# Gate and up, groups 2 to 6: the four down row tiles of a unit stand together behind its fourth product

## The chip, the cores and the metric

The kernel runs on one core of one Trainium2 chip. The metric is the device time of one execution in microseconds. The kernel before takes 769.2 us (median of 3 runs, 769.16 to 769.42). The profiled execution, whose trace is read here, took 769.27 us; its span, from the first to the last instruction that the profile holds, is 767.5 us, so that 1.77 us lie around the span.

The engines are named as the profile names them: PE multiplies matrices and PEld loads the weights for it, DVE and ACT work on vectors in SBUF and PSUM, POOL is the general engine, SP only issues transfers here. Each runs its own instructions strictly in the order in which the program issues them.

## What is computed

Cut to what matters, with one batch of 2048 rows of 448 numbers:

```python
xn = _layernorm(x, axis=-1)
# Fourier mixing: two DFTs as matrix products, the real part kept
a = jnp.einsum("bsd,ed->bse", xn, dft_hid_re)
b = jnp.einsum("bsd,ed->bse", xn, dft_hid_im)
s = jnp.einsum("ts,bse->bte", dft_seq_re, a) - jnp.einsum("ts,bse->bte", dft_seq_im, b)
# gated feed-forward, 448 -> 1792 -> 448
h = (_gelu(xn @ w_gate) * (xn @ w_up)) @ w_down
out = x + s * _silu(h)
```

The change lies in the gated feed-forward.

## The kernel before

Products keep their accuracy by splitting each factor into a high part, rounded to the type that PE reads, and a low part that holds the rest; three products (high by high, high by low, low by high) stand for one (`three`, `two`).

**Stages.** The 1792 hidden columns are cut into 14 tiles of 128, taken in seven groups of two. Group 0 is computed plainly while x is normalised and turned. Groups 1 to 6 run in the loop over `gi`, some 326 us in the middle of the span. After it come the DFT along the hidden dimension and the DFT along the sequence.

**A unit.** In each of the groups 1 to 6 four units follow each other (`bi` from 0 to 3). A unit is one call of `strassen`: one tile of 128 hidden columns for two blocks of 512 rows, gate and up together, by a scheme that forms sums of the weights and of x beforehand and so needs fewer products. Its 39 matmuls on 512 columns are seven products: four on fresh PSUM banks, called `x1` to `x4`, with six matmuls each, and three second parts of five matmuls each, which add to the banks of `x1`, `x3` and `x4`. These four banks are 0 to 3 of the eight, and each unit uses the same ones in the same order, so a unit's `x4` can begin only after the bank has been read by the unit before.

Between the products stand DVE and ACT instructions that move results on. At the end of a unit they form a chain: DVE adds the second part of `x3` (L525) and multiplies by the gelu of `x1` (L526); ACT copies the product as a high part `hs` (L528); DVE forms its low part (L530); DVE adds the second part of `x4` (L534), which is the last reading of that bank; ACT takes the gelu of the sum (L535). What is left (L539 on DVE, L541 on ACT, L544 on DVE) is returned as `late` and issued in the next unit.

**Down row tiles.** The second product, with `w_down`, is spread over later units: eight pieces for each pair of units wait in the queue `dq`, and `send` takes one of them. A piece (`down_one`) is six matmuls on 448 columns into a PSUM bank of the other four (4 to 7), then an ACT copy into `po_out` (L457). Behind the fourth copy POOL issues the transfer that adds `po_out` to `gs` in HBM (L462, 896 KB). `strassen` gets four calls, `dn[0]` to `dn[3]`, and issues them behind its second product, behind its fourth, behind the second part of `x3` and at its end. In the groups 2 to 6 each of them is a `send`.

**Preparation of weights.** `preps` holds four lists of work for later units, issued at four fixed places. In the units `bi` 0 and 3 of the groups 2 to 5, and `bi` 0 of group 6, `preps[1]` and `preps[2]` each split one half of the next weights (`prep_s`): an ACT copy of 896 columns (L356) and DVE subtractions (L358, L362). In the units `bi` 2 they split `w_down` for the next group (an ACT copy L384, then a DVE subtraction L385). `preps[1]` stands behind the fourth product, `preps[2]` behind the gelu of `x1` (L521).

**POOL.** At the beginning of the units `bi` 1 and `bi` 2 of the groups 2 to 5 the program issues `sums_s` on POOL: ten additions and subtractions on 128 columns in SBUF (L338 to L347), which form the sums of the next group's weights. At the end of every third unit `sum_step` has POOL issue two transfers that add DFT matrices in HBM (L809). So what POOL does in its order is: a unit's `gs` transfer, the two transfers of `sum_step` where they are due, and then the ten instructions of the next unit's `sums_s` where it has them. SP loads the raw weights; its load for a raw buffer waits until the buffer's last reader, the DVE subtraction of `preps[2]`, has finished.

Of the kernel before, what the change touches and what calls it, by code (L numbers as in the profile page):

```python
# [45 lines left out]
def fnet_geglu(ctx: ExitStack, tc: tile.TileContext, x, ca, ct, cp, et, wgu, wd, out):  # L46
# [45 lines left out]
    def tmp(i):  # L92
        return a_t[:, 512 * i : 512 * i + 512]
# [7 lines left out]
    def xk(c, k, lo=0):  # L101
        at = k if c % 2 == 0 else (0, 2, 1, 3)[k]
        return a_x[c][:, 2048 * lo + 512 * at :][:, :512]
# [31 lines left out]
    def mm_tile(name):  # L135
        return in_turn("mm", name)
# [162 lines left out]
    def load_s(f, i):  # L299
        raw = a_r[i]  # L300
        nc.sync.dma_start(raw[:, :1280], wgu[f].rearrange("p b f -> p (b f)"))
        return raw
# [108 lines left out]
    def new_hs(f, c):  # L411
        hs_of[f, c] = hs_tile()
        return hs_of[f, c]
# [56 lines left out]
    def three(ps, a, b, first=False):  # L470

        for n, (i, j) in enumerate(((0, 0), (0, 1), (1, 0))):
            nc.tensor.matmul(  # L473
                ps, a[i], b[j], start=first and n == 0, stop=n == 2, skip_group_check=True
            )

    def two(ps, a, b):

        for xt in b:
            nc.tensor.matmul(ps, a[0], xt, start=False, stop=True, skip_group_check=True)  # L480

    def strassen(f, p, w, late, dn, preps):


        c, e = 2 * p, 2 * p + 1
        m, u, g1, c21 = [tmp(i) for i in ((0, 1, 2, 3), (2, 3, 0, 1))[units_n[0] % 2]]
        units_n[0] += 1

        def hl(c, k):
            return xk(c, k), xk(c, k, 1)  # L490

        t, v = t_hl[p]

        def bank(i):
            return mm_tile(f"x{i}_{f}_{p}")

        x1 = bank(1)
        three(x1, w["a11"], hl(c, 0), True)
        three(x1, w["b11"], hl(c, 2))
        nc.scalar.activation(m, x1, AF.Copy)  # L500
        late[0]()
        x2 = bank(2)
        three(x2, w["s2"], t[1], True)
        three(x2, w["r2"], v[1])
        nc.vector.tensor_add(u, m, x2)
        late[1]()
        dn[0]()
        preps[0]()
        x3 = bank(3)
        three(x3, w["s3"], t[2], True)  # L510
        three(x3, w["r3"], v[2])
        nc.vector.tensor_add(m, u, x3)  # L512
        x4 = bank(4)
        three(x4, w["s1"], t[0], True)
        three(x4, w["r1"], v[0])
        nc.vector.tensor_add(m, m, x4)
        preps[1]()
        dn[1]()
        three(x1, w["a12"], hl(c, 1))
        two(x1, w["x2"], hl(c, 3))  # L520
        nc.scalar.activation(g1, x1, AF.Gelu_apprx_tanh)  # L521
        preps[2]()
        three(x3, w["a22"], t[3])
        two(x3, w["x3"], v[3])
        nc.vector.tensor_add(c21, u, x3)  # L525
        nc.vector.tensor_mul(g1, g1, c21)  # L526
        hs = new_hs(f, c)
        nc.scalar.activation(hs[:, 0], g1, AF.Copy)  # L528
        dn[2]()
        nc.vector.tensor_sub(hs[:, 1], g1, hs[:, 0])  # L530
        preps[3]()
        three(x4, w["s4"], hl(e, 1))
        two(x4, w["x4"], hl(e, 3))
        nc.vector.tensor_add(u, u, x4)  # L534
        nc.scalar.activation(u, u, AF.Gelu_apprx_tanh)  # L535
        dn[3]()

        def late0():
            nc.vector.tensor_mul(u, u, m)  # L539
            late0.hs = new_hs(f, e)  # L540
            nc.scalar.activation(late0.hs[:, 0], u, AF.Copy)  # L541

        def late1():
            nc.vector.tensor_sub(late0.hs[:, 1], u, late0.hs[:, 0])  # L544

        return late0, late1

    units_n = [0]


    with tc.manual_schedule():
# [263 lines left out]
        def send():  # L815
            if dq:
                down_one(*dq.pop(0))

        nop = lambda: None

        e_at, e_raw = {}, {}

        def e_load(b):
            e_raw[b] = a_r[0][:, 960 * (b % 2) :][:, : 2 * D]
            nc.sync.dma_start(e_raw[b], et[b].rearrange("p r d -> p (r d)"))
# [17 lines left out]
        for gi in range(1, len(GROUPS)):  # L843
            grp = GROUPS[gi]
            nxt = GROUPS[gi + 1] if gi + 1 < len(GROUPS) else None
            ws = nws
            if gi > 1:
                wdn = nwdn
            nws, n_raw = [None, None], {}
            sides = (0, 0, 1, 1) if gi % 2 else (1, 1, 0, 0)  # L850
            for bi, (i, p) in enumerate(zip((0, 1, 1, 0), sides)):
                preps = [[], [], [], []]
                if gi == 1 and bi == 0:
                    tsp, vsp = t_places(1), v_places(1)
                    preps[0].append(lambda: (comb1.pop(0)(), vsp(3)))
                    preps[2].append(lambda: comb1.pop(0)())
                    preps[3].append(lambda: comb1.pop(0)())
                if gi == 1 and bi == 1:
                    comb1.pop(0)()
                    for n, f, k in ((0, vsp, 1), (1, tsp, 1), (2, tsp, 2), (3, vsp, 2), (3, tsp, 0)):  # L860
                        preps[n].append(lambda f=f, k=k: f(k))
                if gi == 1 and bi == 2:
                    vsp(0)
                    tsp(3)
                if bi == 0:
                    if gi == 1:
                        sums_s(s_raw2, nc.gpsimd)
                        n_raw[-1] = s_raw2
                    else:
                        n_raw[-1] = last_raw  # L870
                    ws[1], steps = prep_s(nw, n_raw[-1])
                    preps[1].append(steps[0])
                    preps[2].append(steps[1])
                    if nxt and gi > 1:
                        n_raw[0] = load_s(nxt[0], 0)
                    elif not nxt:
                        e_load(0)
                        e_load(1)
                elif bi == 1:
                    if nxt:  # L880
                        n_raw[1] = load_s(nxt[1], 1)
                        if gi > 1:
                            n_raw["d"] = load_d(nxt, a_s)
                            sums_s(n_raw[0], nc.gpsimd)
                        else:
                            wdn, steps = prep_d(grp, draw)
                            preps[1] += steps
                    else:
                        E_IN[0] = sb.tile([P, 1920], FR, name="e0", tag="r1")
                        preps[1].append(lambda: (e_split(0, E_IN[0]), e_load(2)))  # L890
                elif bi == 2:
                    if nxt:
                        if gi == 1:
                            n_raw["d"] = load_d(nxt, a_s)
                            n_raw[0] = load_s(nxt[0], 0)
                            sums_s(n_raw[0], nc.gpsimd)
                        sums_s(n_raw[1], nc.gpsimd)
                        nwdn, steps = prep_d(nxt, n_raw["d"])
                        preps[1].append(steps[0])
                        preps[2].append(steps[1])  # L900
                    else:
                        fetch(1)
                        E_IN[1] = sb.tile([P, 4 * D], FR, name="e1", tag="d1")
                        E_IN[2] = sb.tile([P, 2240], FR, name="e2", tag="sp")
                        preps[1].append(lambda: (e_split(1, E_IN[1]), e_load(3)))
                        preps[3].append(lambda: e_split(2, E_IN[2]))
                else:
                    if nxt:
                        nws[0], steps = prep_s(nw, n_raw[0])
                        preps[1].append(steps[0])  # L910
                        preps[2].append(steps[1])
                    else:
                        preps[1].append(lambda: e_split(3, vt[1][:, 7 * D :]))
                dn = [send] * 4
                if gi == 1 and bi < 2:
                    dn = [nop, send, nop, send]
                run = [lambda q=q: [f() for f in q] for q in preps]
                late = strassen(grp[i], p, ws[i], late, dn, run)
                sum_step(4 * gi + bi - 4)
                if bi % 2:  # L920
                    dq += [(gi, c, wdn, kk) for c in (2 * p, 2 * p + 1) for kk in range(4)]
            nw = 1 - nw
            if nxt:
                last_raw = n_raw[1]
# [117 lines left out]
        nxt = {0: 3, 1: 6, 2: 7, 3: 8, 9: None, 10: None}  # L1042
# [366 lines left out]
```

## Time and profile before

| What | Value |
|---|---|
| median of 3 runs | 769.2 us (769.16 to 769.42) |
| profiled execution | 769.27 us |
| its span | 767.5 us |
| granted TensorE clock, mean | 0.999 |
| PEld busy | 686.2 us (89%) |
| DVE busy | 544.4 us (71%) |
| ACT busy | 366.6 us (48%) |
| POOL busy | 179.9 us (23%) |
| all transfers | 170.04 MB, mean 222 GB/s |

A row of a timeline gives the start of an instruction in us from the span's start, its length in us, the engine, the line of the program and what it writes and reads. A row of the chain of waits gives a start, a length and what ran then on the path that ended last. The groups 1 to 6 lie between 71.8 and 397.8 us of the span.

### The profile page before, as it was taken

The numbers are of one execution on the slowest core, as the hardware profiler recorded it, in microseconds if no ns is written. First come the engines' busy times: TensorE is split into PE (matmuls) and PEld (weight loads), VectorE is DVE, ScalarE is ACT, GpSimd is POOL, SyncE is SP. The second block draws the span as 40 slices with busy tenths as digits, with TensorE's granted clock in tenths as the row PEclk, the third lists the DMA queues.
The fourth block names the chain that finished last, engine by engine and source line by source line (L and its number), as shares of the span: only waits on it lengthen the run. The fifth ranks groups of instructions, "written<-read, shape, count | busy, mean of one in ns | idle before, by whom it ended". The sixth has DMA issues, their size and how long they took to land.

```text
span 767.5 us, 11360 instructions
## 1 busy us (share of the span) xinstructions
PE 761.3 (99%) x4054; PEld 686.2 (89%) x4054; DVE 544.4 (71%) x946; ACT 366.6 (48%) x547; POOL 179.9 (23%) x303
## 2 busy tenths in 40 slices
PE   8999999999999999999999999999999999999998
PEld 7988888888888888888889999999999999999997
DVE  7879877555556556455452777978888797979787
ACT  5975554444444344344444585534444444434341
POOL 2204043430501511501011001223222222323130
PEclk9999999999999999999999999999999999999999
DMA  8234458994959968774979981959696969688794
GB/s 298 91 120 150 145 203 172 263 186 104 266 107 252 272 117 225 172 157 84 257 218 240 372 346 54 325 170 334 210 354 205 346 202 343 211 304 268 256 312 153
DMA packets 61513, 170.04 MB, mean 222 GB/s; under 512 B 7440, under 2 KB 40080, under 8 KB 60560
## 3 DMA queue, kind: packets, MB, share of 16 engines
q0 software_dynamic: 13728, 61.02, 35.0%
q1 hardware_dynamic: 34272, 82.48, 30.5%
q10 hardware_dynamic: 13456, 25.81, 9.2%
q8 instruction: 32, 0.52, 0.3%
q14 instruction: 25, 0.20, 0.1%
HBM read 127.21 MB, written 70.91 MB: 258 GB/s over the span
## 4 chain that ended last, share of the span: by engine, by line
PE 99%; DVE 0%; issue 0%; DVEq 0%
PE x L473 24%; PE p L1173 22%; PE po L450 18%; PE p L1176 10%; PE ab L984 9%; PE x L480 4%; PE gu L396 4%; PE py L1188 1%; PE py L1190 1%; PE py L1189 1%; PE gu L599 1%; PE pt L198 1%; PE warm L573 1%; PE p L1206 0%; PE gu L585 0%
## 5 line engine op out<-in xcount | busy, mean ns | idle before, releaser
L473 PE MATMUL x<-xt,w 128*128 128x512 f32 x480 | 149.6, 392 | 0.0
L473 PEld LDWEIGHTS x<-xt,w 128*128 128x128 f32 x480 | 90.1, 188 | 16.3 <-DVE tmp L512 0.7
L457 ACT ACTIVATE po_out<-po 128x448 f32<-128x448 f32 x112 | 60.2, 537 | 81.7 <-PE po L450 79.5
L450 PE MATMUL po<-wd0h,hs 128*128 128x448 f32 x256 | 81.7, 366 | 0.0
L462 POOL DMA_DIRECT2D gs<-po_out x24 | 21.4, 893 | 218.7 <-ACT po_out L457 213.7
L984 PE MATMUL ab<-e,xt 128*128 128x448 f32 x288 | 68.8, 365 | 0.0
L450 PE MATMUL po<-wd,hs 128*128 128x448 f32 x288 | 66.0, 365 | 0.0
L473 PE MATMUL x<-t_v,w 128*128 128x512 f32 x216 | 60.8, 390 | 0.0
L450 PEld LDWEIGHTS po<-wd,hs 128*128 128x128 f32 x288 | 54.1, 188 | 6.7
L984 PEld LDWEIGHTS ab<-e,xt 128*128 128x128 f32 x288 | 54.1, 188 | 4.3
L450 PEld LDWEIGHTS po<-wd0h,hs 128*128 128x128 f32 x256 | 48.1, 188 | 4.9
L473 PEld LDWEIGHTS x<-t_v,w 128*128 128x128 f32 x216 | 40.6, 188 | 8.7
L1064 POOL DMA_DIRECT2D raw<-sums x45 | 24.8, 552 | 94.9 <-DVE xt L143 56.6
L450 PE MATMUL po<-wd0l,hs 128*128 128x448 f32 x128 | 46.9, 367 | 0.0
L142 ACT ACTIVATE e<-raw 128x896 fp32r<-128x896 f32 (+1 forms) x30 | 27.6, 921 | 38.6 <-DVE raw L1071 27.8
L528 ACT ACTIVATE hs<-tmp 128x512 fp32r<-128x512 f32 x24 | 15.2, 634 | 54.6 <-DVE tmp L526 54.6
L473 PE MATMUL x<-t_lo,w 128*128 128x512 f32 x96 | 37.4, 389 | 0.0
L142 ACT ACTIVATE e<-tmp 128x896 fp32r<-128x896 f32 (+1 forms) x22 | 19.7, 896 | 35.7 <-DVE tmp L1071 28.6
L1173 PE MATMUL p<-t_v,wd0l 128*128 128x448 f32 x112 | 36.4, 374 | 0.0
L1173 PE MATMUL p<-w,e 128*128 128x448 f32 x112 | 36.4, 374 | 0.0
L1064 POOL DMA_DIRECT2D tmp<-sums x39 | 21.5, 552 | 59.9 <-DVE xt L143 37.2
L358 DVE TENSOR_TENSOR w<-raw,w 128x512 fp32r<-128x512 f32 (+1 forms) x24 | 21.3, 888 | 18.3 <-ACT w L356 18.3
(374 smaller groups left out, 2017.6 us busy)
## 6 DMA issues: line engine op xcount, KB each, us to landing
gs<-po_out POOLq DMA_DIRECT2D x24, 896.0 KB, 7.8
sums<-ca SPq DMA_DIRECT2D x16, 896.0 KB, 11.2
sums<-ca POOLq DMA_DIRECT2D x16, 896.0 KB, 14.5
t_v<-td ACTq DMA_DIRECT2D x24, 448.0 KB, 5.8
w<-td ACTq DMA_DIRECT2D x24, 448.0 KB, 7.5
raw<-ct SPq DMA_DIRECT2D x45, 192.0 KB, 4.2
raw<-wgu SPq DMA_DIRECT2D x12, 640.0 KB, 5.9
tmp<-ct SPq DMA_DIRECT2D x39, 192.0 KB, 4.6
```

The lines of the kernel that those rows point to most:

```text
L142: nc.scalar.activation(h, src, AF.Copy)
L358: nc.vector.tensor_sub(w[:, 1408 + lo : 1408 + b], raw[:, P + lo : P + b], hw[:, lo:b].bitcast(F32))
L396: nc.tensor.matmul(ps[:, cols], a, xt[:, cols], start=n == 0, stop=n == len(mm) - 1)
L450: nc.tensor.matmul(po[:, :D], hs[:, a, kk * P : (kk + 1) * P], wdn[b][:, i], start=n == 0, stop=n == 5,)
L457: nc.scalar.activation(out_[0][:, kk], po[:, :D], AF.Copy)
L462: nc.gpsimd.dma_start(gv[:, 4 * c : 4 * c + 4], out_[0], accum_op=ALU.add)
L473: nc.tensor.matmul(ps, a[i], b[j], start=first and n == 0, stop=n == 2, skip_group_check=True)
L480: nc.tensor.matmul(ps, a[0], xt, start=False, stop=True, skip_group_check=True)
L984: nc.tensor.matmul(p[:, :D], a, b, start=n == 0, stop=n == len(mm) - 1)
L1064: nc.gpsimd.dma_start(v[:, 4 * P : 6 * P], sums[j][:, KS.index(k)])
L1173: nc.tensor.matmul(ps[q][:, :D], h, v, start=u % UN == 0, stop=False, skip_group_check=True)
L1176: nc.tensor.matmul(ps[q][:, :HD], l, v[:, :HD], start=False, stop=u % UN == NS - 1, skip_group_check=True,)
```

## The change

The calls of `down_one` stay the same in number, kind and order; four of them now stand in one place. In the units concerned `dn[0]`, `dn[2]` and `dn[3]` do nothing and `dn[1]` calls `send` four times, behind the fourth product. Where `dn[0]` is the function `nop`, `preps[2]` is issued ahead of `dn[1]`, right behind `preps[1]`. Group 1 keeps its order (the `lambda: None` in its first units is another function than `nop`, so the test does not hold there), and so do the last three units of group 6. That leaves 17 changed units: all 16 of the groups 2 to 5 and the first of group 6.

```diff
         preps[1]()
+        if dn[0] is nop:
+            preps[2]()
         dn[1]()
         three(x1, w["a12"], hl(c, 1))
         two(x1, w["x2"], hl(c, 3))
         nc.scalar.activation(g1, x1, AF.Gelu_apprx_tanh)
-        preps[2]()
+        if dn[0] is not nop:
+            preps[2]()
...
     units_n = [0]
+    nop = lambda: None
...
-        nop = lambda: None
...
-                dn = [send] * 4
-                if gi == 1 and bi < 2:
-                    dn = [nop, send, nop, send]
+                dn = [nop, lambda: [send() for _ in range(4)], nop, nop]
+                if gi == 1 or (bi and not nxt):
+                    dn = [send] * 4 if gi > 1 or bi > 1 else [lambda: None, send, nop, send]
```

On PE, in the first unit of group 2 (its banks are `x_4_1_1225` for `x1`, then one each for `x2` to `x4`; `po_2_0` to `po_2_3` are its four row tiles), the kernel before has this behind its second product:

```order
L450 MATMUL po_2_0_1244<-wd_78,hs_80 128x448 x3
L450 MATMUL po_2_0_1244<-wd_78,hs_79 128x448 x3
L473 MATMUL x_4_1_1252<-xt_69,w 128x512
L473 MATMUL x_4_1_1252<-t_lo,w 128x512
L473 MATMUL x_4_1_1252<-xt_69,w 128x512
L473 MATMUL x_4_1_1252<-t_v_822,w 128x512 x3
L473 MATMUL x_4_1_1260<-xt_69,w 128x512
L473 MATMUL x_4_1_1260<-t_lo,w 128x512
L473 MATMUL x_4_1_1260<-xt_69,w 128x512
L473 MATMUL x_4_1_1260<-t_v_822,w 128x512 x3
L450 MATMUL po_2_1_1271<-wd_78,hs_80 128x448 x3
L450 MATMUL po_2_1_1271<-wd_78,hs_79 128x448 x3
```

And the changed kernel has this from the last rows of its fourth product on:

```order
L473 MATMUL x_4_1_1252<-xt_69,w 128x512
L473 MATMUL x_4_1_1252<-t_v_822,w 128x512 x3
L450 MATMUL po_2_0_1265<-wd_78,hs_80 128x448 x3
L450 MATMUL po_2_0_1265<-wd_78,hs_79 128x448 x3
L450 MATMUL po_2_1_1273<-wd_78,hs_80 128x448 x3
L450 MATMUL po_2_1_1273<-wd_78,hs_79 128x448 x3
L450 MATMUL po_2_2_1281<-wd_78,hs_80 128x448 x3
L450 MATMUL po_2_2_1281<-wd_78,hs_79 128x448 x3
L450 MATMUL po_2_3_1289<-wd_78,hs_80 128x448 x3
L450 MATMUL po_2_3_1289<-wd_78,hs_79 128x448 x3
L473 MATMUL x_4_1_1225<-xt_68,w 128x512 x3
```

The four groups of six matmuls on 448 columns have become one group of 24; the 24 matmuls of the four fresh products now follow each other, and so do the 15 of the second parts with the 24 of the next unit.

On ACT, in the same unit, from the copy of `x1` to that of the next unit's `x1`, the kernel before has:

```order
L500 ACTIVATE tmp<-x_4_1_1225 128x512
L541 ACTIVATE hs_80<-tmp 128x512
L457 ACTIVATE po_out<-po_2_0_1244 128x448
L356 ACTIVATE w<-raw_75 128x896
L457 ACTIVATE po_out<-po_2_1_1271 128x448
L521 ACTIVATE tmp<-x_4_1_1225 128x512
L356 ACTIVATE w<-raw_75 128x896
L528 ACTIVATE hs_80<-tmp 128x512
L457 ACTIVATE po_out<-po_2_2_1295 128x448
L535 ACTIVATE tmp<-tmp 128x512
L457 ACTIVATE po_out<-po_2_3_1311 128x448
L500 ACTIVATE tmp<-x_5_1_1332 128x512
```

And the changed kernel (the gelu of `x1`, L521 before, is L523 now; L528, L535 and L541 are L531, L538 and L544):

```order
L500 ACTIVATE tmp<-x_4_1_1225 128x512
L544 ACTIVATE hs_80<-tmp 128x512
L356 ACTIVATE w<-raw_75 128x896 x2
L457 ACTIVATE po_out<-po_2_0_1265 128x448
L457 ACTIVATE po_out<-po_2_1_1273 128x448
L457 ACTIVATE po_out<-po_2_2_1281 128x448
L457 ACTIVATE po_out<-po_2_3_1289 128x448
L523 ACTIVATE tmp<-x_4_1_1225 128x512
L531 ACTIVATE hs_80<-tmp 128x512
L538 ACTIVATE tmp<-tmp 128x512
L500 ACTIVATE tmp<-x_5_1_1332 128x512
```

The second copy of weights has moved ahead of all four copies of row tiles, and the fourth copy, for which POOL's `gs` transfer waits, has moved from the end of the unit to a place ahead of the gelu of `x1`.

On POOL the order of instructions is the same in both kernels. This is its piece from the `gs` transfer of the third group's second unit to its `sums_s`, as it stands in both:

```order
L462 DMA gs<-po_out 128x1792
L338 TENSOR_TENSOR raw_75<-raw_75 128x128
L339 TENSOR_TENSOR raw_75<-raw_75 128x128
L340 TENSOR_TENSOR raw_75<-raw_75 128x128
L341 TENSOR_TENSOR raw_75<-raw_75 64x128
L342 TENSOR_TENSOR raw_75<-raw_75 128x128
```

Nothing has moved within POOL's order, nor within those of DVE and SP. What has moved is the ACT copy for which the first of these rows waits.

## The prediction

> **What bounds the kernel now.** I read the page first: the engines' busy time, then the chain that ended last.
>
> ```profile
> PE 761.3 (99%) x4054; PEld 686.2 (89%) x4054; DVE 544.4 (71%) x946; ACT 366.6 (48%) x547; POOL 179.9 (23%) x303
> PE 99%; DVE 0%; issue 0%; DVEq 0%
> ```
>
> PE is the bound everywhere, and it waits for nobody. So this change can gain only what the spacing of matmuls gives, and it loses whatever makes PE wait. The next view is the chain in order of time, for the length of a unit.
>
> ```profile
> 71.78 5.44 PE x L473 x24
> ...
> 108.44 2.74 PE x L473 x12
> ...
> 122.36 2.74 PE x L473 x12
> ...
> 136.14 2.74 PE x L473 x12
> ...
> 149.91 2.74 PE x L473 x12
> ...
> 402.29 4.86 PE po L450 x24
> ```
>
> The units that begin at 122.36 and 136.14 last 13.78 and 13.77 us. Their ideal is in the same rows: 24 matmuls on 512 columns take 5.44 us where nothing stands between (0.2267 each), so 39 take 8.84; 24 on 448 columns in one piece take 4.86. Together 13.70.
>
> **The gain in spacing.** The difference, some 0.07 us, is paid at the changes between the two lengths:
>
> ```profile
> 130.27 0.70 PE x L473 x3
> 130.97 0.46 PE x L480 x2
> 131.42 0.68 PE x L473 x3
> 132.10 0.45 PE x L480 x2
> ```
>
> The five matmuls behind a row tile take 1.16 us, the next five 1.13: a return from 448 to 512 columns costs about 0.03 us, partly given back inside the short row tile. A unit returns four times now and once afterwards. I take 8.84 + 4.86 + 0.03 = 13.73 for the changed unit: 0.04 less. Bounds from the same rows: 0 (if a long piece pays at its end what four short ones pay) to 0.07. 17 units by 0.04 make **0.7 us of gain** (0 to 1.2).
>
> **What else moves.** The matmuls, copies and transfers are the same in number. I place everything in a changed unit by its start on PE: four fresh products to 5.44, row tiles to 10.30, second parts of `x1`, `x3`, `x4` to 11.46, 12.60 and 13.73. The next unit's `x1` needs its bank at 13.73, its `x4` at 13.73 + 4.08 = 17.81. These rows price the rest:
>
> ```profile
> 205.51 0.53 ACT L457 ACTIVATE po_out<-po 128x448 f32<-128x448 f32 x1
> 206.44 0.90 POOL L462 DMA_DIRECT2D gs<-po_out  x1 [5.44 <-ACT po_out L457]
> 207.07 0.77 POOL L338 TENSOR_TENSOR raw<-raw 128x128 f32<-128x128 f32 x1
> ...
> 208.34 0.74 POOL L341 TENSOR_TENSOR raw<-raw 64x128 f32<-64x128 f32 x1
> 208.46 2.84 DVE L544 TENSOR_TENSOR hs<-tmp,hs 128x512 fp32r<-128x512 f32 x1
> ...
> 209.43 0.94 ACT L384 ACTIVATE wd0h<-xf 128x896 fp32r<-128x896 f32 x1
> ...
> 210.01 0.72 POOL L345 TENSOR_TENSOR raw<-raw 128x128 f32<-128x128 f32 x1
> ...
> 214.10 0.60 ACT L521 ACTIVATE tmp<-x 128x512 f32<-128x512 f32 x1 [0.61 <-PE x L480]
> 215.23 0.69 DVE L525 TENSOR_TENSOR tmp<-tmp,x 128x512 f32<-128x512 f32 x1 [1.55 <-PE x L480]
> 216.03 0.69 DVE L526 TENSOR_TENSOR tmp<-tmp 128x512 f32<-128x512 f32 x1
> 216.75 0.64 ACT L528 ACTIVATE hs<-tmp 128x512 fp32r<-128x512 f32 x1 [2.05 <-DVE tmp L526]
> 217.42 0.69 DVE L530 TENSOR_TENSOR hs<-tmp,hs 128x512 fp32r<-128x512 f32 x1 [0.70 <-ACT hs L528]
> ```
>
> *ACT.* The second weight copy (0.94, as L384 on the same size) goes ahead of the row tiles' copies; both fit before the first tile ends at 6.66. A copy (0.53) comes every 1.22 us, so ACT keeps up: the fourth runs from 10.30 to 10.83. The gelu of `x1` starts at 11.46 and ends at 12.06, 1.67 us before PE wants that bank. Cost nothing; if ACT were over 1.5 us late, PE would wait at `x1`. The DVE subtraction behind the moved copy is finished earlier too, and SP's next raw load, which waits for it, starts earlier; nobody is waiting for that load.
>
> *The chain at the unit's end.* Before, two row tiles (2.4 us) of the second parts' time covered it. Now DVE's L525 starts when `x3` ends, 12.60. L526 follows 0.80 later (216.03 less 215.23), to 14.09; L528 14.12 to 14.76; L530 14.79 to 15.48. L534, the last reader of the bank of `x4`, starts 0.61 behind L530's start:
>
> ```profile
> 148.55 0.69 DVE L530 TENSOR_TENSOR hs<-tmp,hs 128x512 fp32r<-128x512 f32 x1 [0.70 <-ACT hs L528]
> 149.16 0.68 DVE L534 TENSOR_TENSOR tmp<-tmp,x 128x512 f32<-128x512 f32 x1
> ```
>
> So it ends at 16.08, and PE may go on some 0.2 later:
>
> ```profile
> 116.62 0.67 DVE L512 TENSOR_TENSOR tmp<-tmp,x 128x512 f32<-128x512 f32 x1
> 117.35 0.19 PEld L473 LDWEIGHTS x<-xt,w 128*128 128x128 f32 x1 [0.28 <-DVE tmp L512]
> 117.35 0.50 PE L473 MATMUL x<-xt,w 128*128 128x512 f32 x1
> ```
>
> Here, in group 1, a weight load did wait for DVE (ended 117.29), and the unit that begins at 108.44 took 13.92 instead of 13.78: released at 117.35 + 0.14 = 117.49. So an undisturbed chain frees the bank at 16.28, 1.53 us before 17.81: hidden, with less cover than before.
>
> *POOL, the term that decides.* POOL's `gs` transfer waits for the fourth copy. Before, that copy stood at the unit's end, and `sums_s` ran early in the next unit. Now L462 starts 0.40 behind 10.83 (206.44 less 206.04), at 11.23, and L338 0.63 later, at 11.86. `sums_s` has moved into the chain. What that does is in the first row block: DVE's L544, which reads two SBUF tiles, came 1.39 us after L338 began and took 2.84 instead of 0.69; it ended 0.57 after L345, 4.23 after L338. L526 and L530 read two SBUF tiles too. L526 now wants to start at 13.40, 1.54 after L338: the same place in POOL's sequence. Priced by that row it ends at 11.86 + 4.23 = 16.09, L528 runs to 16.76, L530 to 17.48, L534 to 18.08, PE is free at 18.28: **0.47 us of wait** at the next `x4`.
>
> This holds at boundaries where the next unit has `sums_s` and no transfers of `sum_step` stand ahead: five of the eight (behind `bi` 0 of groups 2, 4, 5 and `bi` 1 of groups 3, 4). At the other three L338 comes later and begins slowly:
>
> ```profile
> 151.30 0.88 POOL L462 DMA_DIRECT2D gs<-po_out  x1 [6.67 <-ACT po_out L457]
> ...
> 153.00 1.41 POOL L338 TENSOR_TENSOR raw<-raw 128x128 f32<-128x128 f32 x1
> 153.36 0.69 DVE L544 TENSOR_TENSOR hs<-tmp,hs 128x512 fp32r<-128x512 f32 x1
> ...
> 154.48 0.75 POOL L340 TENSOR_TENSOR raw<-raw 128x128 f32<-128x128 f32 x1
> ...
> 156.59 0.71 POOL L345 TENSOR_TENSOR raw<-raw 128x128 f32<-128x128 f32 x1
> ```
>
> 1.70 after L462: 12.93. L526 at 13.40 comes 0.47 behind it, and L544 at 0.36 passed undisturbed, so L526 ends at 14.09 and L530 wants to start at 14.79, 1.86 after L338, when L340 has begun (1.48 after it). If it is held to L345 (4.30 after L338, 17.23) and ends 0.57 later, at 17.80, L534 ends 0.60 after that, PE is free at 18.60: 0.79 us. Bounds for each boundary: 0, if DVE gets in at once, to 2.2, if L526 is held so late too.
>
> The page "SBUF — State Buffer" of the Trainium skill, section "Who interferes with whom", says that a DVE instruction with two SBUF inputs contends with a GpSimd instruction that reads SBUF, and that the loser waits for the whole instruction. The trace agrees that they contend (2.84 for 0.69), but there the wait outlasted five POOL instructions, not one. By the page's lock of one instruction the wait would be 0.4 us and the time that of the second rival.
>
> *Other waits.* Queued behind the held L526 on DVE stand L530, L534 and the next unit's L539, L505, L544 and L512, and through them ACT's L535, L500 and L541. All run some 2 to 3 us late, but of these PE needs L534 first; the others release banks or `tmp` tiles that it wants from the second parts on, at 10.30 of the next unit. The rows of `hs` that the tiles read are complete by 17.48, and the next unit's tiles begin at 13.73 + 5.44. The `gs` transfer starts about 5 us earlier in the unit, so its buffer, needed two units later, is free earlier. Behind `bi` 2 and 3 no `sums_s` follows: no wait there.
>
> **The sum.** 769.27 of the profiled execution (the median is 769.2) − 0.7 + 5 × 0.47 + 3 × 0.79 = 769.27 − 0.7 + 2.35 + 2.37 = **773.3 us**, 0.5% slower. With each wait uncertain by some 0.15 us, this case lies between 772.1 and 774.6.
>
> **Rivals.**
> 1. *Only five boundaries wait.* At the three with transfers L530 slips in. For it:
>
> ```profile
> 112.72 0.47 POOL L339 TENSOR_TENSOR raw<-raw 128x128 f32<-128x128 f32 x1
> 112.78 0.95 DVE L539 TENSOR_TENSOR tmp<-tmp 128x512 f32<-128x512 f32 x1 [0.70 <-ACT tmp L535]
> ```
>
> An arrival during L339 was held only 0.26 us, and 1.86 after a slow L338 is near the end of L339. 769.27 − 0.7 + 2.35 = 770.9.
> 2. *No wait, not slower.* DVE gets in behind one POOL instruction (0.4 us, as in these two rows). The mechanism decides at one point: a chain held less than 1.53 us stays hidden. Then only the spacing is left: 769.27 − 0.7 = 768.6. Against it: L544's 2.84 at nearly the same distance from L338 as L526 will have.
> 3. *Both L526 and L530 meet POOL at the three.* L526 held to 17.80 gives L528 to 18.47, L530 to 19.19, L534 to 19.79, free at 19.99: 2.18 each. 769.27 − 0.7 + 2.35 + 6.54 = 777.5. Against it: the 0.69 of the L544 at 0.36.
> 4. *The order doesn't reach the chip as written.* The rows of the order exclude it, so the only open part is the spacing gain, 0 to 1.2, which is inside the other cases.
>
> **How the numbers follow.** Forecast 773.3: 0.50. Rival 1: 0.17; rival 2: 0.20; rival 3: 0.07; the rest 0.06, half of it a gain beyond 0.2% from spacing I can't see. About 0.2% (1.5 us) is what a measurement of this kernel can tell from no change. Rival 1 lies at that edge, so half of it counts as the same. Faster 0.04, same 0.28, slower 0.68. The range runs from rival 2 to the upper end of the forecast, 768.4 to 774.6, and leaves out 0.13.
>
> **What would show it.** In the changed trace: row tiles as one piece of 24 in 4.86 and undisturbed units of 13.73 (the gain); L338 at 11.9 or 12.9 of the units `bi` 0 and 1; the multiplication (L529 there) or the subtraction behind it taking over 2 us; PEld waiting for DVE's last addition (L537 there) at `x4` of the units `bi` 1 and 2, eight times, 0.4 to 0.9 each; units `bi` 2 to 3 and 3 to 0 without waits. I am wrong if these DVE instructions stay near 0.7 us beside `sums_s`, or if PE waits at `x1` for the gelu instead.

## The result and the profile after

The changed kernel takes 775.56 us (median of 6 runs, 775.42 to 776.08). The kernel before takes 769.20 us beside it, the median of five runs (769.16 to 769.6); a sixth run of it took 1112.59 us and is left out of the comparison. The ratio is 1.0083, with a 95% interval of 1.0072 to 1.0094: 0.8% slower. The forecast was 773.3 us, with a range to 774.6: the sign and the mechanism came out, the size did not.

The page of the changed kernel, its busy times and the chain that ended last by engine:

```profile
PE 763.3 (99%) x4054; PEld 686.0 (89%) x4054; DVE 557.5 (72%) x946; ACT 371.3 (48%) x547; POOL 179.8 (23%) x303
PE 93%; DVE 5%; ACT 1%; issue 0%; DVEq 0%
```

The chain was PE alone; now 5% of it is DVE. These 5% are not the loss: at each boundary, the place where one unit ends and the next begins, the path runs over DVE for some 4.7 us, but PE works through most of that. PE's share of the span still rounds to 99%, for 6 us are 0.8% of it: the share alone would not show them. The view of waits, for the weight loads in the groups 2 to 6 (line, releaser, total us, times, longest), names them:

```profile
PEld x L473 <- DVE tmp L537: 8.2, 8, 1.4
```

Eight waits, all for the last DVE addition of a unit (L537 here, L534 before), as many as there are boundaries with POOL's sums behind them. The chain in order of time (start, length, what; this view leaves out the shortest pieces, among them here ACT's copy L531 and the addition L537):

```profile
122.13 5.46 PE x L473 x24
127.59 4.87 PE po L450 x24
...
134.79 0.70 DVE tmp L528
135.58 2.63 DVE tmp L529
138.90 0.71 DVE hs L533
140.26 1.67 PE x L473 x6
141.93 4.86 PE po L450 x24
...
165.22 5.44 PE x L473 x24
170.66 4.86 PE po L450 x24
...
178.95 5.44 PE x L473 x24
```

The unit from 165.22 to 178.95 has nothing behind it and lasts 13.73 us, 0.04 less than before, with its 24 row tile matmuls in one piece of 4.86. Between the row tiles at 127.59 and those at 141.93, with a boundary between them, lie 14.34 us. How that comes about, by the timeline around this boundary (start, length, engine, line, what it writes and reads, idle time before it and who ended it):

```profile
133.39 0.88 POOL L462 DMA_DIRECT2D gs<-po_out  x1 [7.41 <-ACT po_out L457]
...
133.96 0.79 POOL L338 TENSOR_TENSOR raw<-raw 128x128 f32<-128x128 f32 x1
...
135.58 2.62 DVE L529 TENSOR_TENSOR tmp<-tmp 128x512 f32<-128x512 f32 x1
...
136.93 0.71 POOL L345 TENSOR_TENSOR raw<-raw 128x128 f32<-128x128 f32 x1
...
138.24 0.63 ACT L531 ACTIVATE hs<-tmp 128x512 fp32r<-128x512 f32 x1 [3.98 <-DVE tmp L529]
...
138.90 0.71 DVE L533 TENSOR_TENSOR hs<-tmp,hs 128x512 fp32r<-128x512 f32 x1 [0.70 <-ACT hs L531]
...
139.12 0.84 PE L473 MATMUL x<-t_v,w 128*128 128x512 f32 x3
139.54 0.67 DVE L537 TENSOR_TENSOR tmp<-tmp,x 128x512 f32<-128x512 f32 x1
...
140.26 0.19 PEld L473 LDWEIGHTS x<-xt,w 128*128 128x128 f32 x1 [0.72 <-DVE tmp L537]
140.26 0.50 PE L473 MATMUL x<-xt,w 128*128 128x512 f32 x1 [0.30 <-DVE tmp L537]
...
140.60 0.40 PE L473 MATMUL x<-t_lo,w 128*128 128x512 f32 x1
```

POOL's sums start 0.57 us behind the start of the `gs` transfer, the multiplication L529 comes 1.62 us after L338 and takes 2.62 us instead of 0.69, and ends 0.56 after L345. What follows it is as long as ever. The weight load of the next `x4` stands 0.72 us. Of the other kind of boundary, where two POOL transfers stand ahead of the sums, these rows of the timeline behind the first unit of group 3:

```profile
191.94 1.74 POOL L338 TENSOR_TENSOR raw<-raw 128x128 f32<-128x128 f32 x1
...
192.37 1.73 POOL L339 TENSOR_TENSOR raw<-raw 128x128 f32<-128x128 f32 x1
192.38 0.99 DVE L529 TENSOR_TENSOR tmp<-tmp 128x512 f32<-128x512 f32 x1
...
194.07 3.05 DVE L533 TENSOR_TENSOR hs<-tmp,hs 128x512 fp32r<-128x512 f32 x1 [0.70 <-ACT hs L531]
...
195.85 0.72 POOL L345 TENSOR_TENSOR raw<-raw 128x128 f32<-128x128 f32 x1
...
197.77 0.19 PEld L473 LDWEIGHTS x<-xt,w 128*128 128x128 f32 x1 [1.43 <-DVE tmp L537]
```

There L529 slips through, and the subtraction L533 is held, as forecast; but L529 itself took 0.99, and the slow L338 1.74 instead of 1.41.

### The profile page after: what moved, and what is told of

It reads as the page before. It is cut to its first block, busy times and chain, and to the rows that moved or that the text cites. A ratio compares the mean times of both kernels' runs of the same rounds, so it can differ in the third digit from the quotient of the medians.

```text
span 773.7 us, 11369 instructions
## 1 busy us (share of the span) xinstructions
PE 763.3 (99%) x4054; PEld 686.0 (89%) x4054; DVE 557.5 (72%) x946; ACT 371.3 (48%) x547; POOL 179.8 (23%) x303
## 4 chain that ended last, share of the span: by engine, by line
PE 93%; DVE 5%; ACT 1%; issue 0%; DVEq 0%
PE p L1176 21%; PE x L473 19%; PE po L450 18%; PE p L1179 10%; PE ab L987 9%; PE gu L396 4%; PE x L480 4%; DVE tmp L529 2%; DVE hs L533 2%; PE py L1191 1%; PE py L1193 1%; PE py L1192 1%; PE gu L603 1%; PE pt L198 1%; PE warm L577 1%; DVE tmp L528 1%
## 5 line engine op out<-in xcount | busy, mean ns | idle before, releaser
L450 PE MATMUL po<-wd0h,hs 128*128 128x448 f32 x256 | 78.0, 367 | 0.0
L528 DVE TENSOR_TENSOR tmp<-tmp,x 128x512 f32<-128x512 f32 x24 | 16.5, 686 | 73.4 <-PE x L480 73.4
L450 PE MATMUL po<-wd,hs 128*128 128x448 f32 x288 | 61.8, 365 | 0.0
L531 ACT ACTIVATE hs<-tmp 128x512 fp32r<-128x512 f32 x24 | 15.2, 632 | 61.6 <-DVE tmp L529 61.6
L533 DVE TENSOR_TENSOR hs<-tmp,hs 128x512 fp32r<-128x512 f32 x24 | 25.4, 1057 | 16.8 <-ACT hs L531 16.8
```

What stands on the lines that cost most here:

```text
L450: nc.tensor.matmul(po[:, :D], hs[:, a, kk * P : (kk + 1) * P], wdn[b][:, i], start=n == 0, stop=n == 5,)
```

## The experiments

Their times stand beside the kernel before, run on the same chip. It took 769.08 us beside four of them (all sums held back, transfers ahead, another order, second preparation back) and 769.15 us beside the other three. The changed kernel was not run again beside them: its 775.56 us is that of the first measurement.

**Holding POOL's sums back.** A one-element copy on POOL waits for a DVE result of the running unit, and the sums stand behind it:

```diff
+        def sums_late(raw, hs):
+            nc.gpsimd.tensor_copy(gate, hs[:, 1, :1].bitcast(F32))
+            sums_s(raw, nc.gpsimd)
...
-                            sums_s(n_raw[0], nc.gpsimd)
+                            preps[0].append(lambda r=n_raw[0], v=late: sums_late(r, v[0].hs))
...
-                        sums_s(n_raw[1], nc.gpsimd)
+                        if gi > 1:
+                            preps[0].append(lambda r=n_raw[1], v=late: sums_late(r, v[0].hs))
+                        else:
+                            sums_s(n_raw[1], nc.gpsimd)
```

> The changed kernel, with POOL's ten sums of weights in the units bi 1 and 2 of groups 2 to 5 held back by a one-element POOL copy that reads the low part hs finished some 5 us into the unit; nothing else moves. Theory A (the end-of-unit chain on DVE is held by POOL's sums): the eight waits of the weight load for L537 vanish, L529 and L533 take 0.7 us, all changed units last 13.73 us, and the time is 775.56 - 7.1 = 768.5 us, 0.1% under the kernel before. Theory B (the chain is late of itself, because the second parts of the products now follow each other without row tiles between, or because of the gs transfer that now starts there): the eight waits stay, 775.5 us.

Measured: 768.44 us, 0.9993 of before (0.9984 to 1.0002), and no wait of a weight load in the groups 2 to 6. The timeline at the same boundary behind the first unit of group 3:

```profile
189.01 2.00 POOL L813 DMA_DIRECT2D sums<-ca  x2
...
190.55 0.69 DVE L529 TENSOR_TENSOR tmp<-tmp 128x512 f32<-128x512 f32 x1
...
191.94 0.69 DVE L533 TENSOR_TENSOR hs<-tmp,hs 128x512 fp32r<-128x512 f32 x1 [0.70 <-ACT hs L531]
...
196.08 0.19 POOL L848 COPY gate<-hs 128x1 f32<-128x1 f32 x1 [5.07 <-DVE hs L547]
...
196.22 0.46 POOL L338 TENSOR_TENSOR raw<-raw 128x128 f32<-128x128 f32 x1
```

The transfers still run at that place, and L529 and L533 take 0.69 beside them. So neither the transfers nor the closer order of the products makes the waits; the sums do. Theory B falls.

**Holding back half of them.** Only the first line of that edit, for the sums behind the units `bi` 0.

> The changed kernel, with only the sums that run behind the units bi 0 held back (those issued at the start of bi 1 of groups 2 to 5); those behind bi 1 stay in the chain. Theory A: the four waits in the units bi 1 vanish (0.59, 1.28, 0.65 and 0.63 us in the changed kernel), the four in the units bi 2 stay: 775.56 - 3.15 = 772.4 us. If the waits had a common cause beside the sums, the time would not fall by just these four.

Measured: 772.71 us, 1.0045 of before (1.0031 to 1.0059), and 2.85 less than the changed kernel for 3.15 expected; the view of waits for the weight loads of the groups 2 to 6:

```profile
PEld x L473 <- DVE tmp L537: 4.4, 4, 1.4
```

Four waits are gone and four stay. In the two traces the last unit of group 6 starts 3.27 us earlier; some 0.4 us of that is lost again behind the groups; why is open. The waits add up boundary by boundary.

**The DFT sums' transfers ahead of the unit.**

```diff
-        def sum_step(at):
+        def sum_step(at, which=(0, 2)):
...
-            for d in (0, 2):
+            for d in which:
...
+                ahead = dn[0] is nop
+                if ahead:
+                    sum_step(4 * gi + bi - 4, (2,))
                 late = strassen(grp[i], p, ws[i], late, dn, run)
-                sum_step(4 * gi + bi - 4)
+                sum_step(4 * gi + bi - 4, (0,) if ahead else (0, 2))
```

> The changed kernel, with the two POOL transfers of sum_step issued ahead of a changed unit instead of behind it, so that none stand between the gs transfer and the sums. Theory A: the three boundaries with 1.28 us of wait become like the other five (some 0.65 us each), because L338 starts at 11.8 of the unit and not at 12.9, L529 instead of L533 is held, and no slow L338 adds its 0.3 us: 775.56 - 3 x 0.63 = 773.7 us. Theory B': the longer wait of these three comes from the DFT sums' transfers loading the DMA queues: it stays 1.28, 775.5 us.

Measured: 773.65 us, 1.0059 of before (1.0045 to 1.0073). The view of waits for the weight loads, as above, and the timeline behind the first unit of group 3:

```profile
PEld x L473 <- DVE tmp L537: 6.3, 8, 0.8
```

```profile
190.25 0.81 POOL L338 TENSOR_TENSOR raw<-raw 128x128 f32<-128x128 f32 x1
...
191.80 2.70 DVE L529 TENSOR_TENSOR tmp<-tmp 128x512 f32<-128x512 f32 x1
```

Still eight waits, but the longest is 0.8 instead of 1.4: without the transfers L338 is as quick as elsewhere, and this boundary is like the other five. The edit takes the transfers away from this place and lets the sums begin earlier, so by itself it does not part the two. The first experiment speaks for the sums: there the transfers run at their old place, and L529 and L533 take 0.69 beside them. Whether the transfers slow the sums themselves is not shown.

**The same sums in another order.** In the kernel's order only the last two of the ten depend on the one just before; here seven do, because they read its result or overwrite what it reads.

```diff
         eng.tensor_sub(s3, g0, u0)
-        eng.tensor_sub(s7, g2, u2)
         eng.tensor_add(u0, u0, u1)
-        eng.tensor_add(u2[:64], u2[:64], u3[:64])
         eng.tensor_sub(s2, u0, g0)
-        eng.tensor_sub(s6, u2, g2)
         eng.tensor_sub(s4, g1, s2)
+        eng.tensor_sub(s7, g2, u2)
+        eng.tensor_add(u2[:64], u2[:64], u3[:64])
+        eng.tensor_sub(s6, u2, g2)
         eng.tensor_sub(u2d, g2d, u2d)
```

> The changed kernel, with the ten sums of weights in another order, so that all but two of them need the result of the one just before; same work, same place. Theory A1 (DVE is shut out only by a stream of POOL instructions that run into each other, and gets in at the first gap): the first gap comes after one or two instructions, L529 and L533 are held under 1 us each, the waits fall under 0.2 us: 768.5 to 769.5 us. Theory A2 (POOL keeps the port for the whole series whatever its gaps): waits of 0.6 to 1.3 us stay, 775 to 776 us.

Measured: 768.34 us, 0.9989 of before (0.9980 to 0.9998): the best kernel here, and faster than the kernel before by just about what can be told. No weight load waits in the groups 2 to 6. The timeline behind the first unit of group 4:

```profile
244.68 0.46 POOL L339 TENSOR_TENSOR raw<-raw 128x128 f32<-128x128 f32 x1
...
245.22 0.46 POOL L340 TENSOR_TENSOR raw<-raw 128x128 f32<-128x128 f32 x1
...
245.34 0.89 DVE L529 TENSOR_TENSOR tmp<-tmp 128x512 f32<-128x512 f32 x1
...
245.77 0.79 POOL L341 TENSOR_TENSOR raw<-raw 128x128 f32<-128x128 f32 x1
...
246.52 0.46 POOL L342 TENSOR_TENSOR raw<-raw 128x128 f32<-128x128 f32 x1
...
246.93 0.69 DVE L533 TENSOR_TENSOR hs<-tmp,hs 128x512 fp32r<-128x512 f32 x1 [0.70 <-ACT hs L531]
247.06 0.89 POOL L343 TENSOR_TENSOR raw<-raw 64x128 f32<-64x128 f32 x1
```

L339, L340 and L341 now lie 0.54 to 0.55 apart with 0.08 between them, and the sums run in the middle of the chain as they do in the changed kernel. L529 arrives during L340, is held 0.2 us and gets in ahead of L341, which takes 0.79 instead of 0.46.

Is that gain the new order's own? The kernel before, with this order and nothing else:

> The kernel before, with the ten sums in the chained order and nothing else. The order of the sums alone should be worth nothing in the units of groups 2 to 6 (no wait there to remove): 769.1 us, the same as the kernel before; at most 0.3 us less from group 1, where DVE was held at L530 and L544. If instead it comes out at 768.3 us, the gain of the chained run was not the regrouping's.

Measured: 769.1 us, 0.9998 of before (0.9989 to 1.0007). The order alone is worth nothing that can be measured; it is worth 7.2 us where the row tiles stand together. Its effect on DVE shows here too: the L544 that took 2.84 us in the trace before, 1.39 behind L338, comes at the same distance and takes 0.69:

```profile
208.28 0.69 DVE L544 TENSOR_TENSOR hs<-tmp,hs 128x512 fp32r<-128x512 f32 x1
```

**The second preparation back in its place**, the row tiles still together:

```diff
         preps[1]()
-        if dn[0] is nop:
-            preps[2]()
         dn[1]()
...
-        if dn[0] is not nop:
-            preps[2]()
+        preps[2]()
```

> The changed kernel, with the second preparation of weights back behind the gelu of x1 in all units; the four row tiles stay together. Theory A: in the units bi 0 the DVE subtraction of weights (two SBUF inputs, wanted at 13.0 of the unit) now meets POOL's sums and stands ahead of the whole chain in DVE's order: the waits behind bi 0 grow from 0.65 and 1.28 to some 2.4 us each, with a part of them at x3 (its bank is read by L525); behind bi 3 a wait of about 0.1 us appears: 775.56 + 3 x 1.75 + 1.2 + 0.4 = 782 us. Rival: the preparation's place costs nothing, because the sums hold the chain to the same end anyway: 775.5 us.

Measured: 782.34 us, 1.0171 of before (1.0152 to 1.0190). The view of waits for the weight loads, and two rows of the timeline behind the first unit of group 2:

```profile
PEld x L473 <- DVE tmp L534: 8.8, 8, 2.8
PEld x L473 <- DVE w L358: 6.3, 3, 2.1
```

```profile
135.12 3.46 DVE L358 TENSOR_TENSOR w<-raw,w 128x896 fp32r<-128x896 f32 x1 [5.62 <-ACT w L356]
...
138.64 0.30 PEld L473 LDWEIGHTS x<-xt,w 128*128 128x128 f32 x2 [2.05 <-DVE w L358]
```

The weights' subtraction, 1.09 us undisturbed, is now the one that is held, ahead of the whole chain in DVE's order. The time came out as expected, but one of the waits did not: at three boundaries PE stands first at the sixth matmul of the next unit's `x1`, which needs the weights that L358 forms, and then again at `x4`; the bank of `x3` had been named for the first of these. Behind `bi` 3 no wait appears (0.1 was expected). So the preparation's move, priced at nothing in the prediction, is worth 6.8 us once the tiles stand together.

**The change without any sums behind it**, in nine units:

```diff
-                if gi == 1 or (bi and not nxt):
+                if gi == 1 or (bi and not nxt) or (nxt and bi < 2):
```

> The change in nine units only: bi 2 and 3 of groups 2 to 5 and bi 0 of group 6, none of which has sums of weights behind it; the units bi 0 and 1 of groups 2 to 5 as in the kernel before. Theory A: no waits, each of the nine units 0.04 us shorter: 0.36 us under the kernel before, 768.7 to 768.9 us. If standing together had a cost of its own beside the sums, the time would be above the kernel before.

Measured: 768.86 us, 0.9995 of before (0.9986 to 1.0003). The gain of 0.29 us is near the 0.36 that nine times 0.04 let expect, but within what the measurement can't tell from nothing. What carries the spacing term is the trace: every undisturbed changed unit in all these runs lasts 13.73 to 13.75 us, against 13.77 before.

## Why the prediction was wrong in size

**Spacing.** Right: 13.73 us for the unit as worked out, and 768.34 and 768.44 us where it stands alone (768.6 forecast, as the second rival's time).

**Where the waits are.** Right: eight, at `x4` of the units `bi` 1 and 2, none elsewhere; L529 held at five boundaries, L533 at three. Rivals 1 and 2 let DVE in behind one POOL instruction; it waited until a series of them had passed.

**When DVE is done at the five.** Nearly right: at the boundary shown, L537 ends at 140.21, which is 18.08 after the start of the unit at 122.13 on the scale of the chain, as forecast. At the other four it ends 18.10 to 18.18 after the unit's start, less what that unit was itself delayed: over the five 0.05 late on average.

**The term that was mis-sized at all eight: when PE asks.** The prediction put the need of `x4` at 17.81 and added 0.2 for the release, 0.47 us in all. The five cost 0.59 to 0.71, 0.65 on average: 0.18 more each. 17.81 is on the scale of the chain, in which a piece of PE begins where the matmul before *ends*. But a matmul lasts 0.39 at a spacing of 0.23, so the next one starts 0.16 before that, and its weight load, which does the waiting, about one spacing earlier still. The rows above show it: the load stood idle from 140.26 − 0.72 = 139.54, and its matmul was due at 139.80 (139.12 and three spacings), 17.67 after the unit's start and not 17.81. The matmul behind that one is at 140.60 in the trace, so the late one went on at 140.37, 0.16 after L537's end: 0.57 late, and 0.02 more at the return to speed. The release of 0.2 had been about right. In sum 0.14 for the earlier need, less 0.04 for the release, and 0.02: 0.12 at every boundary, 1.0 us over the eight. DVE's 0.05 at the five adds 0.3.

**The term that was mis-sized at three: how L529 fares beside L338.** It was taken as undisturbed (0.69), as L544 had been in the trace before, which came 0.36 after L338. L529 came 0.44 after it, and in these 0.08 us L339 had started; it took 0.99, L338 1.74 instead of 1.41, and the whole series came later. L345 ends 4.63 after L338 instead of 4.30, L533 with it, and L537 is done 0.36 later than forecast. That it is L339 which held L529, the fourth experiment shows at the same boundary. There L339 stays back for L338, and L529 at the same distance takes 0.69:

```profile
189.97 1.44 POOL L338 TENSOR_TENSOR raw<-raw 128x128 f32<-128x128 f32 x1
190.41 0.69 DVE L529 TENSOR_TENSOR tmp<-tmp 128x512 f32<-128x512 f32 x1
...
191.48 0.46 POOL L339 TENSOR_TENSOR raw<-raw 128x128 f32<-128x128 f32 x1
```

The nearer row was in the prediction: its 0.95 of L539 at 112.78, just behind the start of an L339. The three boundaries cost 1.27 to 1.28 us instead of 0.79; 0.12 of that is the term above, and the rest, 0.36 to 0.37 at each, makes 1.1 us of the error. In the third experiment, where L529 comes some 1.5 us after L338, these three cost 0.67 to 0.71.

Together 4.72 + 1.0 + 0.3 + 1.1 = 7.1; the eight units are longer than 13.73 by 7.08 in sum. With 0.7 us of gain that gives +6.4; the spans differ by 773.7 − 767.5 = 6.2. Most of the rest is in group 1, where the unit that took 13.92 us before takes 13.77 in the profiled execution of the changed kernel.

**The preparation.** It was costed at nothing and hidden, which is right as long as it stands ahead of the tiles; the prediction did not say what its old place would have cost. Its remark that the `gs` transfer starts about 5 us earlier in the unit was too much: 133.39 − 122.13 = 11.26 against 151.30 − 136.14 = 15.16, so 3.9. Nothing in the sum hung on it.

**The range.** It let each wait vary by 0.15 us, all of it as if it were chance. The errors went one way at every boundary, 0.18 at five and 0.49 at three, 2.4 us in all, where the range left 1.3 above the forecast.

## What to carry to other kernels

A step that is moved on one engine can shift work on another whose own order does not change: here a copy's new place started POOL's sums 4 us earlier, into a DVE chain, and that cost ten times the gain of the regrouping. Look at every queue that waits for what is moved, and ask which of its instructions hold up those of the chain. Take the time at which PE needs a tile from the starts of its weight loads and matmuls, not from the ends that a merged chain shows; and where two engines hold each other up, as POOL and DVE do here, an order of work in which each instruction waits for the one before lets the other engine in. Here that cost nothing that could be measured (769.1 against 769.15 us) and was worth 7.2 us.

## What the runs showed of the hardware

A DVE instruction with two SBUF inputs (128x512, 0.69 us alone) waited for a whole run of POOL instructions, issued 0.42 us apart and overlapping: for the one in flight and four to five more, 1.9 to 2.4 us in all, until one of them had to wait for the one before (L346 for L345). Where it came ahead of the second instruction of the run, it was held 0.15 us at most (L544 in the trace before, 0.16 to 0.36 after L338: 0.84 to 0.69), and just behind that one's start 0.3 us (L529, 0.44 after L338: 0.99). With the same POOL instructions in the order in which most wait for the one before, it was held 0.2 us at most. DVE instructions that read one input from PSUM were not held: beside the sums L528 took 0.69 us and L537 0.67. What in the chip makes a run of POOL instructions act as one is not shown.

"SBUF — State Buffer" of the Trainium skill, section "Who interferes with whom", has the pair and the kinds of instruction as these traces show them. That the loser waits for the one instruction of the winner fits the chained order here; in the kernel's own order the wait outlasted the instruction in flight by four to five more.

Alternating between matmuls on 512 and on 448 columns costs some 0.04 us for each unit of four returns against one (13.77 against 13.73 us): small, but the same in every unit.
